# Attention and a Fourier layer on one core: 57 sums of two raw blocks by adding transfers from GpSimd

## The chip, the cores and the metric

One core of a Trainium2 chip runs the whole program. The time is device microseconds (us) for one execution; the program's three runs give 2825.47, 2827.83 and 2831.37 us, median 2827.83.

## What is computed

Two independent layers share the input size (2048 positions, 1024 channels) and are written side by side. All is float32.

```
qkv = x @ wqkv                      # 2048x1024 @ 1024x3072, 32 heads of 32
p   = softmax(q k^T / sqrt(32))     # per head, 2048 x 2048
a   = (p v, heads joined) @ wo      # 2048x1024 @ 1024x1024
u,w = xb @ Wd_re^T, xb @ Wd_im^T    # Fourier layer: along the channels
b   = Ws_re @ u - Ws_im @ w         # along the positions, real part
out = concat(a, b)
```

## The kernel before

**Matmuls.** TensorE (PE) does three products for one float32 product: each operand is split in a high and a low part (float32r), and high x high, low x high and high x low are added in PSUM. `halves` makes the split: line 544 (DVE) or 542 (ACT) copies the block to the high part, line 547 (GpSimd, POOL in the profile, or DVE) subtracts to get the low part. A stationary operand of four 128 x 128 blocks is a piece, tile `hl`, four buffers (`piece`); a moving operand is a tile `slot` (`moving`).

**Seven products in place of eight.** All large products except attention's own are cut 2 x 2 and made by seven block products (numbered 1 to 7) of sums and differences of blocks. So a piece is often a sum of raw blocks: product 5 of the query/key/value stage needs w10 + w11, product 6 needs w10 + w11 - w00. `fetch` makes these sums: it loads the first block into a tile `raw` (or `er`, ten buffers, in the opening; line 506), loads each further block into a second tile (`g`, or `raw` in the opening; line 515), and adds or subtracts it in place with an instruction on POOL or DVE (line 522). Where a later product uses the sum again, it is stored (line 531).

**Stages.** The opening (`qkv`, the first 200 us) makes queries, keys and values of the first three pairs of weight blocks by products 1, 2, 5, 6, 3 in turn; each product takes six groups of 12 matmuls for queries and keys, then eight for values. Results of product 5 are stored group by group (`u_d`, line 820) on SP's queue. Then attention of 32 heads runs from about 210 us to about 2747 us in three streams on PE: S (scores, line 1896, for row maxima on DVE, line 1902, and row sums on ACT, line 1905), T (transposed scores, line 2018, exponentials on ACT, line 2022) and V (line 2037). The rest of the projections and the whole Fourier layer are cut into groups of matmuls, the fills (line 457), that PE does between the streams' steps; the last of them are a tail after attention.

**Who sets the order.** `Plan` simulates the five engines with a cost for every operation (`op`) and lets each engine take, by rank, what is ready. An operation that may run on POOL or DVE goes where it is begun first. POOL's operations and DVE's two-input ones or casts are kept from running at the same time, as the plan reckons. The plan is run 90 times with drawn parameters, and the shortest is written out as each engine's instruction order. On the chip every queue is in order: an instruction that waits holds those behind it. All transfers of before are issued by SP but one; a load that must wait for a buffer, or a store that waits for its result, holds the loads behind it.

**Small rows.** For each head, `scores` makes the row maxima's high and low parts in a tile `lh`, transposes them into `lt` and stores them; both have two buffers.

Of the kernel before, what the change touches and what calls it, by code (L numbers as in the profile page):

```python
# [9 lines left out]
F32 = mybir.dt.float32  # L10
F32R = mybir.dt.float32r
AF = mybir.ActivationFunctionType
ALU = mybir.AluOpType
# [4 lines left out]
P = 128  # L18
# [5 lines left out]
NS = S // P  # L24
# [39 lines left out]
class Plan:  # L64
# [49 lines left out]
    def op(self, engine, cost, emit, after=(), uses=(), rank=0.0, kb=0, order=None, other=None, lanes=1, two=False, wide=False):  # L114

        o = Op(engine, cost, emit, rank, kb, other, two)
        o.lanes, o.wide = lanes, wide
        self.ops.append(o)  # L120
        seen = set()
        for d in after:
            if d is not None and id(d) not in seen:
                seen.add(id(d))
                self._wait(o, d)
        for u in uses:
            u.append(o)
        if order is not None:
            p, order.first = order.first, o
            if p is not None and not p.begun:  # L130
                p.soon.append(o)
                o.left += 1
        return o
# [18 lines left out]
    def start(self, o, e=None):  # L152
        e = e or o.engine
        ins = None
        if not self.dry:
            o.emit(e) if o.other else o.emit()
            ins = self.tc.nc.cur_bb.bb.instructions[-1]
        if not self.dry and e == "POOL" and self.ported[0] > self.now - self.BEHIND:
            self.tc.add_manual_dep(ins, self.ported[1].name, mybir.DependencyInfo(mybir.DependencyClass.Sync, mybir.DependencyReason.DATA), reason="shared port")
        if e == "DVE" and o.two:  # L160
            self.ported = (self.now + (o.cost if e == o.engine else o.other[1]), ins)
        o.begun = True
        self.free[e] = self.now + (o.cost if e == o.engine else o.other[1])
        if e == "POOL" or e == "DVE" and o.two:
            self.port = self.free[e]
        if o.kb:
            for _ in range(o.lanes):
                t = max(self.free[e], self.lane[0])
                self.dma = max(self.dma, t) + o.kb / o.lanes / self.KB_US * (self.WIDE if o.wide else 1.0)
                o.end = self.dma + self.LANDING  # L170
                self.lane = self.lane[1:] + [o.end]
                if o.lanes > 1:
                    self.free[e] = t + o.cost
        else:
            o.end = self.free[e]
            self.free[e] -= self.OVERLAP.get(e, 0.0)
        for t in o.then:
            t.ready = max(t.ready, self.after(o, e, t))
            t.left -= 1
            if t.left == 0:  # L180
                self._release(t)
        for t in o.soon:
            t.ready = max(t.ready, self.now)
            t.left -= 1
            if t.left == 0:
                self._release(t)
# [67 lines left out]
def kernel(  # L254
# [12 lines left out]
    nc = tc.nc  # L267
# [77 lines left out]
    sm = ctx.enter_context(tc.tile_pool(name="sm", bufs=1, reuse_waits="tile"))  # L345
# [42 lines left out]
    MAX, EVAC, CAST, BIT = 1.22, 0.685, 0.415, 0.275  # L388
    SUB = 1.31
    ISSUE = 0.46  # L390

    LATE = 0.25
    HB = 0
# [20 lines left out]
    op = pl.op  # L414
# [69 lines left out]
    def fetch(shape, terms, store=None, keep=None):  # L484

        box = {}
        raws, seconds, tile_of, gate = where[0]
        rank = seq()
        sign, *first = terms[0]
        loaded = len(first) == 2  # L490
        if len(terms) == 1 and not loaded:
            return first[0].get, first[0].made, first[0].users
        if keep is None:
            old, users = raws.take()
        else:

            old, users = gate + keep.users, keep.users

        def dest():
            if "r" not in box:  # L500
                box["r"] = tile_of(shape, "raw", len(raws.users)) if keep is None else keep.get()
            return box["r"]

        last = None
        if loaded:
            last = op("SP", ISSUE, lambda: nc.sync.dma_start(dest(), first[0]), old + first[1] + gate, [users], rank, 256, raws if keep is None else None)
            old = []
        for sign, *term in terms[1:]:
            other = {}
            if len(term) == 2:  # L510
                gold, gusers = seconds.take()

                def load(src=term[0], other=other):
                    other["q"] = tile_of(shape, "g", len(seconds.users))
                    nc.sync.dma_start(other["q"], src)

                q = op("SP", ISSUE, load, gold + term[1] + gate, [gusers], rank, 256, seconds)
            else:
                other["k"], q, gusers = term[0], term[0].made, term[0].users

            def add(e, sign=sign, other=other, a=None if last is not None else first[0]):
                (nc.gpsimd if e == "POOL" else nc.vector).tensor_tensor(  # L522
                    out=dest(), in0=dest() if a is None else a.get(), in1=other["q"] if "q" in other else other["k"].get(), op=ALU.add if sign > 0 else ALU.subtract)

            last = op("POOL", SUB, add, old + [first[0].made if last is None else last, q], [users, gusers] + ([first[0].users] if last is None else []),
                      rank, 0, raws if keep is None and last is None else None, other=("DVE", ADD, 20 + rank), two=True)
            old = []
        if keep is not None:
            keep.made = last
        if store is not None:  # L530
            store[1].append(op("SP", ISSUE, lambda: nc.sync.dma_start(store[0], dest()), [last], [users], rank, 256))
        return dest, last, users
# [1326 lines left out]

    streams = {n: [] for n in "STV"}  # L1860
    psS_r, psT_r, pt_r, vt_r, rt_r, ot_r = Ring(2), Ring(2), Ring(NPT), Ring(2), Ring(1), Ring(2)
    small = {n: Ring(b) for n, b in (("st", 2), ("nm", 2), ("lh", 2), ("tw", 1))}
    qx_r = Ring(1)
    got = {}
    Tops, Sops = {}, {}
# [6 lines left out]
    def scores(h):  # L1872
# [12 lines left out]
        for n, (qt, c) in enumerate([(k % 4, k // 4) for k in range(8)] + [divmod(k, 2) for k in range(8, 32)]):  # L1885
            old, users = psS_r.take()
            own = h > 0 and qt < 4
            box = {}
# [20 lines left out]
            b = op("DVE", MAX, mx, [a] + (sold if n == 0 else []), [users, suse], 0)  # L1909
            e = op("ACT", ES, ex, [b], [users, suse], 0)  # L1910
# [10 lines left out]
        box = {}  # L1921
# [3 lines left out]
            nc.vector.tensor_reduce(out=ST["nm"], in_=ST["negm"].rearrange("p c n -> p n c"), axis=AX.X, op=ALU.min)  # L1925

        def high():
            box["l"] = sm.tile([P, 2, NS], F32R, name="lh", bufs=2)
            nc.vector.tensor_reduce(out=box["l"][:, 0], in_=ST["negm"].rearrange("p c n -> p n c"), axis=AX.X, op=ALU.min)

        def low():
# [3 lines left out]
        a = op("DVE", TINY, nmin, maxes + nold, [nuse, suse], -2)  # L1935
        c = op("DVE", TINY, low, [a, b], [nuse, luse], -2, two=True)
        def across():
            box["t"] = sm.tile([P, 2 * NS], F32, name="lt", bufs=2)
            nc.vector.transpose(box["t"], f(box["l"]).rearrange("p i s -> p (i s)"))

        d = op("DVE", TINY, across, [b, c], [luse], -2)
# [291 lines left out]
```

## Time and profile before

| | |
|---|---|
| three runs, median (range) | 2827.83 us (2825.47 to 2831.37) |
| profiled execution, first to last instruction | 2829.8 us |
| PE busy | 2797.1 us (99%) |
| DVE busy | 2377.2 us (84%) |
| ACT busy | 2355.6 us (83%) |
| POOL busy | 1191.7 us (42%) |
| transfers | 768.18 MB, mean 271 GB/s |

Matmuls are pipelined, so PE's busy time also hides some that start late; the distance between the starts of matmuls tells more. Waits are put down to what came last by the profile. The profiled execution has no other time than its span.

### The profile page before, as it was taken

How to read it: one execution, taken by the hardware profiler on the slowest of the kernel's cores; microseconds unless marked ns; L12 is line 12 of the kernel's file. 1: busy time of each engine (PE TensorE's matmuls, PEld its weight loads, DVE VectorE, ACT ScalarE, POOL GpSimd, SP SyncE). 2: the span in 40 equal slices, each digit the busy share in tenths (PEclk: the TensorE clock that was granted, in tenths of full speed). 3: DMA queues.
4: the chain of work that ended last, by engine and by line, in shares of the span. 5: the costliest groups of instructions: out<-in, count | busy, mean ns of one | idle time of the engine just before them, and what ended most of it. 6: DMA issues, size and time to landing. Idle time of an engine off the chain costs nothing.

```text
span 2829.8 us, 47069 instructions
## 1 busy us (share of the span) xinstructions
PE 2797.1 (99%) x14728; PEld 2095.6 (74%) x14728; DVE 2377.2 (84%) x3300; ACT 2355.6 (83%) x4490; POOL 1191.7 (42%) x945
## 2 busy tenths in 40 slices
PE   9999999999999999999999999999999999999999
PEld 8787777776777777677676777767767777777777
DVE  6678888788888888798988899888888998888845
ACT  5348898998899899889999988999988988888851
POOL 2234434133234432356545446676765331343300
PEclk9999999999999999999999999999999999999999
DMA  9989978798899988977999767888867665677548
GB/s 345 344 312 305 316 249 293 252 337 298 300 302 344 333 298 297 296 232 231 335 342 339 251 207 241 293 270 266 277 179 237 220 211 185 203 237 252 178 154 296
DMA packets 485844, 768.18 MB, mean 271 GB/s; under 512 B 120382, under 2 KB 153406, under 8 KB 485470
## 3 DMA queue, kind: packets, MB, share of 16 engines
q1 hardware_dynamic: 485452, 765.04, 81.6%
q8 instruction: 119, 1.95, 0.3%
q14 instruction: 129, 1.06, 0.1%
q10 hardware_dynamic: 144, 0.13, 0.0%
HBM read 511.74 MB, written 253.25 MB: 270 GB/s over the span
## 4 chain that ended last, share of the span: by engine, by line
PE 88%; DMA 5%; ACT 3%; DVE 2%; issue 1%; POOL 1%; SPq 1%; DVEq 0%; POOLq 0%; ACTq 0%
PE pd L457 40%; PE pd L2037 15%; PE psT L2018 15%; PE psS L1896 14%; PE psT L457 4%; ACT psS L1905 2%; ACT pt L2022 1%; DVE negm L1902 1%; DMA ha_d<-slot 1%; DMA ha_d<-c 0%; DMA c<-in_xb 0%; DMA raw<-in_xa 0%; DMA slot<-in_ct 0%; DMA qs<-qk_d 0%; DMA raw<-in_wv 0%
## 5 line engine op out<-in xcount | busy, mean ns | idle before, releaser
L457 PE MATMUL pd<-slot,hl 128*128 128x512 f32 x5088 | 1412.1, 380 | 4.0 <-ACT hl L542 2.0
L2022 ACT ACTIVATE pt<-psT 128x512 f32<-128x512 f32 x2048 | 1215.3, 689 | 228.8 <-PE psT L2018 227.3
L1902 DVE TENSOR_REDUCE negm<-psS 128x1 f32<-128x1024 f32 x1024 | 1241.5, 1219 | 169.2 <-PE psS L1896 153.8
L1905 ACT ACTIVATE psS<-psS,negm 128x1024 f32<-128x1024 f32 x1024 | 1225.1, 1197 | 41.6 <-DVE negm L1902 40.7
L457 PEld LDWEIGHTS pd<-slot,hl 128*128 128x128 f32 x5088 | 963.8, 190 | 133.3 <-ACT hl L542 2.4
L2018 PE MATMUL psT<-qs,ks 128*128 128x512 f32 x2048 | 786.0, 387 | 1.2 <-DMA r_d<-ll 0.7
L2018 PEld LDWEIGHTS psT<-qs,ks 128*128 128x128 f32 x2048 | 383.2, 188 | 168.8 <-issue 46.9
L1896 PE MATMUL psS<-ks,qs 128*128 128x512 f32 x1552 | 457.9, 381 | 9.1 <-ACT psS L1905 8.9
L2037 PE MATMUL pd<-pt,vt 128*32 128x512 f32 x4096 | 459.3, 594 | 2.8 <-DVE e L766 1.8
L547 POOL TENSOR_TENSOR slot<-raw,slot 128x512 fp32r<-128x512 f32 x153 | 194.9, 1279 | 353.8 <-DVE slot L547 98.8
L547 POOL TENSOR_TENSOR slot<-slot,slot 128x512 fp32r<-128x512 f32 x206 | 260.4, 1280 | 196.3 <-DVE slot L544 50.1
L1896 PEld LDWEIGHTS psS<-ks,qs 128*128 128x128 f32 x1552 | 283.7, 189 | 66.4 <-ACT psS L1905 21.3
L2037 PEld LDWEIGHTS pd<-pt,vt 128*32 128x32 f32 x4096 | 123.9, 110 | 281.4 <-issue 261.3
L1905 ACT ACTIVATION_READ_ACCUMULATOR psS<-psS,negm 128x1 f32 x1024 | 324.8, 317 | 0.0
L522 POOL TENSOR_TENSOR raw<-raw,g 128x512 f32<-128x512 f32 x114 | 145.4, 1279 | 231.9 <-DMA g<-tg_d 23.6
L547 POOL TENSOR_TENSOR hl<-raw,hl 128x512 fp32r<-128x512 f32 x113 | 144.4, 1279 | 214.8 <-PE psT L2018 62.0
L457 PE MATMUL pd<-slot,slot 128*128 128x512 f32 x780 | 200.8, 379 | 0.0
L457 PEld LDWEIGHTS pd<-slot,slot 128*128 128x128 f32 x780 | 147.4, 189 | 20.1
L1896 PE MATMUL psS<-ks,qx 128*128 128x512 f32 x496 | 146.5, 386 | 6.1 <-ACT psS L1905 5.3
L1896 PEld LDWEIGHTS psS<-ks,qx 128*128 128x128 f32 x496 | 90.0, 189 | 34.9 <-ACT psS L1905 10.9
L522 DVE TENSOR_TENSOR raw<-raw,g 128x512 f32<-128x512 f32 x146 | 106.9, 740 | 9.1 <-issue 2.2
L2050 DVE TENSOR_TENSOR ot<-ot,pd 128x512 f32<-128x512 f32 x64 | 43.9, 686 | 68.7 <-PE pd L2037 67.9
(139 smaller groups left out, 2135.0 us busy)
## 6 DMA issues: line engine op xcount, KB each, us to landing
hl<-ha_d SPq DMA_DIRECT2D x134, 512.0 KB
slot<-in_ct SPq DMA_DIRECT2D x144, 256.0 KB
qk_d<-e SPq DMA_DIRECT2D x52, 512.0 KB
qs<-qk_d SPq DMA_DIRECT2D x128, 192.0 KB
ks<-qk_d SPq DMA_DIRECT2D x128, 192.0 KB
raw<-g_d SPq DMA_DIRECT2D x96, 256.0 KB
ha_d<-hl SPq DMA_DIRECT2D x42, 512.0 KB
raw<-in_ct SPq DMA_DIRECT2D x80, 256.0 KB
```

The costliest lines, as they stand in the source:

```text
L457: nc.tensor.matmul(box["ps"], a[1]((a[0].hi, a[0].lo)[u]()), turns((b[0].hi, b[0].lo)[v]()), start=k == 0, stop=k == n - 1)
L522: (nc.gpsimd if e == "POOL" else nc.vector).tensor_tensor(out=dest(), in0=dest() if a is None else a.get(), in1=other["q"] if "q" in other ...
L547: (nc.gpsimd if e == "POOL" else nc.vector).tensor_tensor(out=lo(), in0=raw(), in1=f(hi()), op=ALU.subtract)
L1896: nc.tensor.matmul(p[:, i * NB : i * NB + NB], (QX[0] if own else QS[h % 2])[:, qt * P : qt * P + P], turns(KS[h % 2][:, c * 1024 + i * NB ...
L1902: nc.vector.tensor_reduce(out=ST["negm"][:, c, qt : qt + 1], in_=box["p"], axis=AX.X, op=ALU.max, negate=True)
L1905: nc.scalar.activation(box["p"], box["p"], AF.Exp, bias=ST["negm"][:, c, qt : qt + 1], accum_out=ST["sums"][:, c, qt : qt + 1])
L2018: nc.tensor.matmul(box["p"], KS[h % 2][:, t * P : t * P + P], turns(QS[h % 2][:, j * NB : j * NB + NB]), start=True, stop=True)
L2022: nc.scalar.activation(box["t"], box["p"], AF.Exp)
L2037: nc.tensor.matmul(po["p"][j * DH : j * DH + DH, :], VT[h][:, k, :], box["t"], start=(k == t0), stop=(k == t), tile_position=(0, j * DH),)
L2050: nc.vector.tensor_tensor(out=as_two(po["o"]), in0=as_two(po["o"]), in1=order_of(po["p"]), op=ALU.add)
```

## The change

```diff
@@ Plan.start
-            t.ready = max(t.ready, self.after(o, e, t))
+            t.ready = max(t.ready, self.after(o, "SP" if o.kb else e, t))
...
+    ADDING = 1.0
...
@@ fetch
         for sign, *term in terms[1:]:
             other = {}
+            if len(term) == 2 and sign > 0 and last is not None:
+                last = op("POOL", ADDING, lambda src=term[0]: nc.gpsimd.dma_start(dest(), src, accum_op=ALU.add), [last] + term[1] + gate, [users], rank, 256)
+                continue
             if len(term) == 2:
                 gold, gusers = seconds.take()
...
-    small = {n: Ring(b) for n, b in (("st", 2), ("nm", 2), ("lh", 2), ("tw", 1))}
+    small = {n: Ring(b) for n, b in (("st", 2), ("nm", 2), ("lh", 1), ("tw", 1))}
...
-            box["l"] = sm.tile([P, 2, NS], F32R, name="lh", bufs=2)
+            box["l"] = sm.tile([P, 2, NS], F32R, name="lh", bufs=1)
...
-            box["t"] = sm.tile([P, 2 * NS], F32, name="lt", bufs=2)
+            box["t"] = sm.tile([P, 2 * NS], F32, name="lt", bufs=1)
...
-    nc = bacc.Bacc("TRN2", target_bir_lowering=False, num_devices=1, dynamic_dma_scratch_size=256)
+    nc = bacc.Bacc("TRN2", target_bir_lowering=False, num_devices=1, dynamic_dma_scratch_size=512)
```

In `fetch`, a further block that is loaded and added (not subtracted, and not the first of the sum) no longer goes to a second tile. Once the first block has landed, GpSimd issues a transfer that adds the second block to what lies in the tile. The plan takes 1.0 us of POOL for the issue and gives the transfer the same landing time as one of SP's. 57 sums fit: 24 of the query/key/value weights (14 of them in the opening: eight of the value weights, six of the query/key weights), 8 of the Fourier layer's input, 9 of the last projection and 16 in the Fourier layer's last stage. `lh` and `lt` have one buffer, and the scratch for descriptors that GpSimd writes has 512 bytes a partition, not 256. As the plan reckons with other operations, all engines' orders change; in the changed program lines after 390 stand one lower, after 509 four lower (506 becomes 507, 515 becomes 519, 522 becomes 526, 531 becomes 535, 547 becomes 551, 820 becomes 824), and the adding transfers are line 512.

POOL's queue early in the opening, before; `er` are sums' tiles, `slot` and `hl` low parts of operands, `e` and `vh` the two parts of a finished query/key block:

```order
L547 TENSOR_TENSOR slot3_1016<-er_953,slot3_1016 128x512
L547 TENSOR_TENSOR slot36_1263<-er_1198,slot36_1263 128x512
L522 TENSOR_TENSOR er_1244<-er_1244,raw_1227 128x512
L522 TENSOR_TENSOR er_1268<-er_1268,raw_1258 128x512
L547 TENSOR_TENSOR e_1323<-e_1323,vh_1331 128x512
L547 TENSOR_TENSOR slot39_1347<-er_1268,slot39_1347 128x512
L522 TENSOR_TENSOR er_1446<-er_1446,raw_1334 128x512
L522 TENSOR_TENSOR er_1462<-er_1462,raw_1453 128x512
L547 TENSOR_TENSOR slot1_1533<-er_1462,slot1_1533 128x512
```

and after:

```order
L551 TENSOR_TENSOR slot3_1016<-er_953,slot3_1016 128x512
L512 DMA er_1191<-in_wv 128x512
L512 DMA er_1198<-in_wv 128x512
L512 DMA er_1209<-in_wv 128x512
L551 TENSOR_TENSOR e_1268<-e_1268,vh_1275 128x512
L512 DMA er_1216<-in_wv 128x512
L551 TENSOR_TENSOR slot36_1303<-er_1191,slot36_1303 128x512
L551 TENSOR_TENSOR slot37_1319<-er_1198,slot37_1319 128x512
L551 TENSOR_TENSOR slot39_1355<-er_1216,slot39_1355 128x512
L512 DMA er_1227<-in_wqk 128x512
```

Before, POOL makes two of product 5's value-weight sums (er_1244, er_1268), DVE the others. Now all four are adding transfers, three of them ahead of the low part of `e`.

POOL's queue at product 6 before, whose three query/key pieces are er_1854, er_1931 and er_1972 (the rows name their last subtraction, POOL's share):

```order
L522 TENSOR_TENSOR er_1734<-er_1734,raw_1762 128x512
L547 TENSOR_TENSOR slot13_1831<-er_1734,slot13_1831 128x512
L547 TENSOR_TENSOR slot15_1906<-er_1817,slot15_1906 128x512
L522 TENSOR_TENSOR er_1854<-er_1854,raw_1883 128x512
L522 TENSOR_TENSOR er_1931<-er_1931,raw_1904 128x512
L522 TENSOR_TENSOR er_1972<-er_1972,raw_1950 128x512
L547 TENSOR_TENSOR hl_2049<-er_1972,hl_2049 128x512
L522 TENSOR_TENSOR er_2064<-er_2064,raw_2057 128x512
```

and after, where the pieces are er_1792, er_1901 and er_1938:

```order
L551 TENSOR_TENSOR slot7_1717<-er_1660,slot7_1717 128x512
L512 DMA er_1683<-in_wv 128x512
L512 DMA er_1712<-in_wv 128x512
L512 DMA er_1747<-in_wv 128x512
L512 DMA er_1777<-in_wv 128x512
L512 DMA er_1792<-in_wqk 128x512
L551 TENSOR_TENSOR hl_1905<-er_1792,hl_1905 128x512
L512 DMA er_1901<-in_wqk 128x512
L512 DMA er_1938<-in_wqk 128x512
```

Five adding transfers, four of value weights and one for the first piece, now stand in a row ahead of the first piece's low part; its subtraction has gone to DVE.

SP's queue at the second piece of product 6 (er_1931) before; u_d20 to u_d23 are stores of product 5's groups, one each 12 matmuls:

```order
L820 DMA u_d21_2_592<-e_1878 128x512
L506 DMA er_1894<-in_xa 128x512
L515 DMA raw_1904<-in_wqk 128x512
L531 DMA sv_d3_512<-er_1817 128x512
L820 DMA u_d22_2_595<-e_1900 128x512
L506 DMA er_1921<-in_xa 128x512
L820 DMA u_d23_2_598<-e_1923 128x512
L515 DMA raw_1929<-in_wqk 128x512
L506 DMA er_1931<-in_wqk 128x512
```

and after (er_1901):

```order
L824 DMA u_d21_2_592<-e_1855 128x512
L507 DMA er_1872<-in_xa 128x512
L507 DMA er_1881<-in_xa 128x512
L824 DMA u_d22_2_595<-e_1878 128x512
L535 DMA sv_d3_512<-er_1777 128x512
L507 DMA er_1901<-in_wqk 128x512
L535 DMA sq_d0_501<-er_1792 128x512
L824 DMA u_d23_2_598<-e_1903 128x512
L519 DMA raw_1913<-in_wqk 128x512
```

The load of the second piece's base and one of the two loads of activations (in_xa) now stand ahead of the next u_d store. The first piece's base (er_1792) stands ahead of u_d18, where before (er_1854) it stood behind u_d19, ahead of u_d20; the third's base stands last ahead of the store u_d0_4 in both.

## Prediction

> **What bounds the kernel now.** I read the page first, then the waits of PE, then PE's stretches, then the timeline and the chain of waits around the one stretch of the program's opening in which PE falls back.
>
> ```profile
> span 2829.8 us, 47069 instructions
> PE 2797.1 (99%) x14728; PEld 2095.6 (74%) x14728; DVE 2377.2 (84%) x3300; ACT 2355.6 (83%) x4490; POOL 1191.7 (42%) x945
> ```
>
> PE is the bound: all that any edit outside PE can win is 2829.8 - 2797.1 = 32.7 us of recorded idle time, and what hides in matmuls that run late. The waits of PE name who ended that idle time (total, times, longest):
>
> ```profile
> PE psS L1896 <- ACT psS L1905: 14.2, 23, 2.6
> PE pd L457 <- ACT hl L542: 2.0, 1, 2.0
> PE pd L2037 <- DVE e L766: 1.8, 1, 1.8
> ...
> PE psT L457 <- DVE hl L547: 1.3, 1, 1.3
> PE pd L457 <- POOL hl L547: 1.0, 1, 1.0
> ```
>
> Most of it, 14.2 us, is attention's own loop: a score block waits until ACT has emptied the last one. Raw sums have no part in that. The three rows that end in hl (a weight piece, split in high and low) do: those pieces are what the 57 sums make. They stand in one place, as the stretches show (PE, PEld, DVE, ACT, POOL busy; clock, DMA share, GB/s):
>
> ```profile
> 50.00:100.00 50.00, 50.00 (x233) 43.80 (x232) 35.55 (x48) 17.40 (x30) 12.56 (x10) 1.00 0.97 341
> 100.00:150.00 50.00, 45.45 (x198) 38.12 (x198) 31.81 (x50) 15.30 (x26) 14.34 (x12) 0.97 1.01 351
> 150.00:200.00 50.00, 50.00 (x234) 43.77 (x233) 35.71 (x48) 21.89 (x37) 13.16 (x10) 1.00 0.97 338
> 2700.00:2750.00 50.00, 50.00 (x293) 34.64 (x290) 20.68 (x33) 29.17 (x54) 0.00 (x0) 1.00 0.37 120
> ```
>
> Around 100 to 150 us PE starts 198 matmuls where its neighbours start 233 and 234, with the transfer engines at 0.97 to 1.01 and 338 to 351 GB/s: the opening is as near to transfer-bound as to PE-bound. PE's timeline there (start, length, last the idle time and what ended it):
>
> ```profile
> 109.09 5.34 PE L457 MATMUL psT<-slot,slot 128*128 128x512 f32 x24
> 114.27 2.75 PE L457 MATMUL pd<-slot,slot 128*128 128x512 f32 x12
> 119.02 0.48 PE L457 MATMUL pd<-slot,hl 128*128 128x512 f32 x1 [1.99 <-ACT hl L542]
> 119.83 4.33 PE L457 MATMUL pd<-slot,hl 128*128 128x512 f32 x11 [0.33 <-DVE hl L547]
> 123.99 3.20 PE L457 MATMUL psT<-slot,hl 128*128 128x512 f32 x13
> 128.46 2.64 PE L457 MATMUL psT<-slot,hl 128*128 128x512 f32 x11 [1.27 <-DVE hl L547]
> 130.94 2.97 PE L457 MATMUL pd<-slot,hl 128*128 128x512 f32 x13
> 134.87 2.64 PE L457 MATMUL pd<-slot,hl 128*128 128x512 f32 x11 [0.96 <-POOL hl L547]
> 137.34 2.75 PE L457 MATMUL psT<-slot,hl 128*128 128x512 f32 x12
> ```
>
> Undisturbed, 24 matmuls take 114.27 - 109.09 = 5.18 us, 0.216 each. From 114.27 to 137.34 there are 72 of them: 15.5 us of work in 23.1, so 7.5 us are lost. This is product 6, whose three weight pieces are sums of three blocks. Each of its first additions becomes an adding transfer. It is the one place where the change touches the path that sets the end.
>
> **The change part by part.** *Removed: 57 additions.* They stand in these groups, with others that stay (mean ns of one behind the busy time):
>
> ```profile
> L522 POOL TENSOR_TENSOR raw<-raw,g 128x512 f32<-128x512 f32 x114 | 145.4, 1279 | 231.9 <-DMA g<-tg_d 23.6 <-DVE raw L522 20.4 <-DVE slot L544 16.2
> L522 DVE TENSOR_TENSOR raw<-raw,g 128x512 f32<-128x512 f32 x146 | 106.9, 740 | 9.1 <-issue 2.2 <-DMA raw<-in_wd 1.4 <-DMA raw<-in_xb 1.4
> L522 DVE TENSOR_TENSOR er<-er,raw 128x512 f32<-128x512 f32 x31 | 24.4, 790 | 2.8 <-DMA er<-in_xa 1.0 <-DMA raw<-in_wv 0.8 <-POOL er L522 0.4
> L522 POOL TENSOR_TENSOR er<-er,raw 128x512 f32<-128x512 f32 x13 | 16.6, 1280 | 44.1 <-DMA er<-in_xa 11.4 <-DVE slot L547 9.4 <-DVE er L522 7.0
> ```
>
> At 0.740 on DVE or 1.279 on GpSimd they are 42 to 73 us of busy time. On the path that is next to nothing: if DVE had all 42 of its 2377.2, it would be 1.8% less busy, and 1.8% of the 14.2 us that scores wait behind DVE and ACT is 0.3 us. I take -0.3.
>
> *Moved: 57 issues, from SP to GpSimd.* The issues of one kind of load, and the casts of such tiles on DVE (min/median/max ns, first and last start):
>
> ```profile
> L506 SPq DMA_DIRECT2D er<-in_wv x20: 327/414/981, 5.0 to 135.9; - x20
> L544 DVE CAST slot<-er x7: 417/426/427, 13.7 to 127.4; 128x512 fp32r<-128x512 f32 x7
> ```
>
> SP gets 57 x 0.414 = 24 us back, 14 x 0.414 = 5.8 of them in the opening. SP waits there for stores (the chain below), so I cost this at nothing; what it does is let loads move ahead, counted below. GpSimd gets 57 issues. No row shows a transfer that GpSimd issues. Its bounds are SP's 0.41 and GpSimd's own whole addition, 1.28; I take 1.0, nearer the row of the engine that does it. That is 57 us where the additions would have been up to 73: GpSimd, at 42%, does not become a bound. Its queue is in order, though. The three transfers that now stand together early on hold up the low half of a finished query/key block, for which a store and then the first scores wait; PE has projection matmuls in hand then, so that costs nothing. The five before the first product 6 piece's low half hold up that half; it needs the fifth of them anyway.
>
> The Trainium skill (SBUF — State Buffer, section "SBUF: two separate sides") says that GpSimd cannot write a transfer's descriptors while DVE runs a two-port copy or cast, which speaks against this change. No run here shows it. In this kernel's rows it would hold one issue by at most a cast, 0.43 us, so 1.3 us for the three pieces of product 6.
>
> *Lengthened: each sum's chain.* Before, two loads fly side by side and an addition follows. Now one load lands, GpSimd issues, and a second flight follows. Flights, from the chain of waits (start, length):
>
> ```profile
> 102.58 4.13 DMA raw<-in_wv
> 107.75 2.71 DMA raw<-in_wv
> ...
> 112.56 0.33 SPq L820
> 112.93 4.86 DMA er<-in_xa
> ...
> 189.91 5.88 DMA raw<-in_xa
> ...
> 200.23 2.52 DMA c<-in_xb
> ```
>
> Bounds 2.5 and 5.9; I take 3.9, the mean of the three within the crowded 100 to 115 us. The chain grows by 1.0 + 3.9 - 1.28 = 3.6 us (bounds 0.41 + 2.52 - 1.28 = 1.7 and 1.28 + 5.88 - 0.74 = 6.4).
>
> The Trainium skill (DMA: Bandwidth & Descriptors, section "Anatomy of one DMA — SWDGE (gpsimd) path") gives 2.0 us and bytes / 436e3 for such a transfer, an estimate of 2.6 us for 256 KB. The quiet flights here, 2.5 and 2.7, agree; the crowded ones do not, and they decide. By that rule the chain would grow by 1.3, not 3.6, and the sum below would come out at -1.9 us (0.0 in place of +2.3).
>
> *Where 3.6 us meets slack.* Product 5's third piece:
>
> ```profile
> 78.41 0.64 SPq L506 DMA_DIRECT2D er<-in_wqk  x1
> 83.96 1.28 POOL L522 TENSOR_TENSOR er<-er,raw 128x512 f32<-128x512 f32 x1 [3.88 <-DVE slot L547]
> 86.48 0.62 ACT L542 ACTIVATE hl<-er 128x512 fp32r<-128x512 f32 x1
> 87.22 0.68 DVE L547 TENSOR_TENSOR hl<-er,hl 128x512 fp32r<-128x512 f32 x1
> 88.37 5.34 PE L457 MATMUL psT<-slot,hl 128*128 128x512 f32 x24
> ```
>
> It is ready at 87.90, and PE needs it halfway through the last row, at 88.37 + 12 x 0.216 = 90.96: slack 3.1. Its load loses one neighbour on SP (0.4). So 3.6 is just covered, 6.4 would cost 2.9.
>
> Product 6 has no slack; PE waits for all three pieces. By the order, the first piece's base load moves ahead across two u_d stores, that is two groups of 12 matmuls, 5.2 us; the second's across one, 2.6 us; the third stays before the same store. So the pieces come 3.6 - 5.2 = -1.6, 3.6 - 2.6 = +1.0 and +3.6 us later. These are not added: a wait for one gives the next its time. I take the middle of the last two, +2.3. An activation load also moves ahead across a store. The chain shows such a load (112.93) as what ended the first wait, 1.99 + 0.33 us. It goes; late next is the first piece, 1.6 earlier. That is worth -1.6.
>
> The other 43 sums are hidden: all of PE's waits for an hl piece (4.3 us in the rows above) lie in the 100 to 150 us stretch, so later sums are ready in time. In the tail, with 16 of them, PE has no idle time at 2700 to 2750 and transfers fill 0.37 of it. Six raw buffers there are six pieces of 2.6 us each ahead, against 3.6. Were that cover gone, the stage would start 3.6 us late, once.
>
> *Single copies* of the two row buffers: a head comes every 2829.8 / 32 = 88 us, and the store that must land first flies at most 5.9. Nothing.
>
> Sum: -0.3 + 2.3 - 1.6 = +0.4 us on 2829.8. The profiled execution is its span, 2829.8 us, 2.0 above the median of the runs and within their spread; I carry the difference over: 2827.83 + 0.4 = **2828.2**.
>
> **The rivals.** *A, the opening's hole closes.* Loads start earlier and need fewer buffers; if that feeds product 6 in time, the 7.5 us come back: 2820.3. For it: the loads' new places. Against: the same bytes cross at 338 to 351 GB/s, and adding transfers come on top. Chance 0.15.
>
> *B, adding transfers are slow in the crowded opening.* They also read what lies in SBUF. If that takes engine time like a second transfer, each costs 262,144 B / 345 GB/s = 0.76 us more, 14 of them 10.6 in a stage without room. Or the chain grows by the upper bound: 6.4 at product 6 and 2.9 at product 5, less the 1.9 gained, 7.4 together. I price it between the two, at 9.0: 2836.8. It decides from issue plus flight of about 7.5 us on: the growth g is then 6.2, and the losses (g - 1.3) + (g - 3.5), less 1.9, are 5.7. For it: no cover at product 6. Against: 3 of the 14 lie on the path. Chance 0.20.
>
> *C, the change does little and the new order does the rest.* The planner reckons every time anew, so all five engines' orders shift, far from any sum. The 23 waits of attention, 14.2 us, then fall elsewhere; half of them more or less is 7.1 us: 2820.7 or 2834.9. Chance 0.10 faster and 0.08 slower.
>
> **How the numbers follow.** What is left, 0.47, is the forecast. Its own range is 2822.5 to 2834, the 0.2% (5.7 us) that a measurement of this kernel, whose runs spread over 5.9 us, can tell from no change. Faster: A and C, 0.25. Slower: B and C, 0.28. The range goes from A's 2820 to just past B's, 2838.
>
> **What would show it.** Right: the hole at 114 to 137 us still there, 6 to 11 us deep, its pieces waiting for a transfer that GpSimd issued; GpSimd's issues near 1 us; landings 2.5 to 6 us later; PE's other waits within a few us of 14.2. Wrong: PE without idle time before 140 us (A); issue plus flight over 7.5 us, waits for adding transfers at product 5 or in the tail (B); attention's waits changed by over 5 us (C).

## The result: 85 us slower

| | before | after |
|---|---|---|
| median (range), four runs each | 2828.15 us (2825.47 to 2831.37) | 2913.05 us (2911.62 to 2914.87) |
| profiled execution, span | 2829.8 us | 2910.2 us |
| PE busy, mean granted clock | 2797.1 us, 0.998 | 2822.9 us, 0.991 |

The ratio is 1.0296 (95% interval 1.0283 to 1.0308). The forecast was 2828.2 us in a range of 2820 to 2838, so the result lies far outside it. The page after, first the span and the engines:

```profile
span 2910.2 us, 47016 instructions
PE 2822.9 (97%) x14728; PEld 2106.3 (72%) x14728; DVE 2380.9 (82%) x3267; ACT 2367.3 (81%) x4506; POOL 1191.4 (41%) x962
```

The span is 80.4 us longer. PE's idle time went from 32.7 to 2910.2 - 2822.9 = 87.3 us, 54.6 more. The other 25.8 are busy time: the same 14728 matmuls took longer. The granted clock fell by 0.7%, which is 20 of 2823 us. The waits of PE after, by line (total, times, longest):

```profile
PE psS L1900 <- ACT psS L1909: 23.8, 31, 3.4
PE pd L458 <- ACT hl L546: 13.1, 1, 13.1
PE psT L2022 <- ACT pt L2026: 10.3, 4, 5.2
PE psT L2022 <- DMA qs<-m_d: 7.6, 4, 3.5
```

One wait for a weight piece (hl) grew from 2.0 to 13.1 us, and attention's waits for its own scores, exponentials and row maxima grew too, though attention has no raw sums. The place tells more than the releaser. Five stretches of PE's time before (PE, PEld, DVE, ACT, POOL busy; clock, DMA share, GB/s):

```profile
0.00:100.00 100.00, 98.54 (x442) 85.53 (x443) 71.36 (x105) 48.87 (x83) 22.20 (x21) 1.00 0.98 344
100.00:200.00 100.00, 95.45 (x430) 81.90 (x430) 67.52 (x97) 37.19 (x62) 27.50 (x22) 0.98 0.99 345
300.00:400.00 100.00, 98.47 (x524) 73.60 (x517) 85.48 (x119) 87.03 (x169) 39.83 (x32) 1.00 0.85 280
900.00:1000.00 100.00, 100.00 (x543) 74.76 (x542) 88.02 (x116) 88.90 (x171) 42.70 (x34) 1.00 0.98 341
2700.00:2800.00 100.00, 100.00 (x524) 78.43 (x521) 47.89 (x75) 41.35 (x74) 1.28 (x1) 1.00 0.59 192
```

The same five after:

```profile
0.00:100.00 100.00, 92.90 (x407) 79.44 (x408) 63.68 (x92) 46.63 (x81) 23.68 (x24) 0.98 0.95 322
100.00:200.00 100.00, 82.06 (x352) 69.65 (x351) 53.02 (x78) 28.70 (x47) 25.87 (x22) 0.90 0.93 289
300.00:400.00 100.00, 88.49 (x466) 61.64 (x455) 76.58 (x105) 75.62 (x146) 41.03 (x35) 0.97 0.89 281
900.00:1000.00 100.00, 90.69 (x452) 67.03 (x453) 85.40 (x110) 81.49 (x155) 36.95 (x31) 0.95 0.94 309
2700.00:2800.00 100.00, 89.81 (x467) 62.69 (x466) 59.66 (x82) 66.08 (x127) 28.66 (x27) 0.95 0.60 141
```

PE's idle time in these 500 us is 56.05 us after and 7.54 before: 48.5 of the 54.6 us. Of all stretches of 100 us only these five have a clock below 1.00. Adding transfers stand in each of them, though also in places that lose less (2249 to 2332 us). Two groups of the adding line (ns min/median/max, first and last start), then what their engine waited for and their landing:

```profile
L512 POOL DMA_DIRECT2D raw<-s_d x16: 872/888/903, 2681.4 to 2772.3; - x16
L512 POOL DMA_DIRECT2D raw<-in_wqk x10: 865/880/1140, 280.7 to 396.2; - x10
...
  issue: 79.0, 19
...
DMA to landing us min/median/max: 3.9/5.0/7.5
```

Issue (0.89) and landing (5.0 with the issue) are as forecast, 1.0 and 4.9. New is "issue: 79.0, 19": 19 times GpSimd stood, 4.2 us each, at an adding transfer for which nothing in the profile was missing. That row shows only a part, since other waits are put down to whatever the profile saw last. By the starts and landings in the trace, 35 of the 57 adding transfers begin 0.26 to 0.32 us after the one before has landed, with 137.4 us of GpSimd's idle time ahead of them, and none begins earlier. GpSimd's timeline in the opening shows it (start, length, last the idle time before it and what ended it):

```profile
105.33 0.89 POOL L512 DMA_DIRECT2D er<-in_wv  x1
111.56 0.87 POOL L512 DMA_DIRECT2D er<-in_wv  x1 [5.34 <-DVE acc L718]
118.50 0.88 POOL L512 DMA_DIRECT2D er<-in_wv  x1 [6.06 <-issue]
124.08 1.00 POOL L512 DMA_DIRECT2D er<-in_wv  x1 [4.70 <-issue]
130.97 0.88 POOL L512 DMA_DIRECT2D er<-in_wqk  x1 [5.89 <-issue]
137.88 1.26 POOL L551 TENSOR_TENSOR hl<-er,hl 128x512 fp32r<-128x512 f32 x1 [6.02 <-ACT hl L546]
```

And PE's there, the hole of product 6:

```profile
122.00 2.75 PE L458 MATMUL pd<-slot,slot 128*128 128x512 f32 x12
137.85 0.80 PE L458 MATMUL pd<-slot,hl 128*128 128x512 f32 x1 [13.10 <-ACT hl L546]
139.19 4.42 PE L458 MATMUL pd<-slot,hl 128*128 128x512 f32 x11 [0.55 <-POOL hl L551]
...
150.13 5.70 PE L458 MATMUL psT<-slot,hl 128*128 128x512 f32 x12 [3.92 <-DVE hl L548]
```

Adding transfers begin 5.6 to 6.9 us apart, each 0.31 or 0.32 us after the one before has landed. The fifth in this line, which begins at 130.97, is the first piece of product 6; PE waits 13.10 us for it. After waits PE is near half speed: the twelve matmuls behind the wait of 3.92 us take 5.70 us, where twelve took 2.75 before the hole. From 130 to 140 us the clock granted to PE is 0.50.

### The profile page after: what moved, and what is told of

It is laid out like the page before. It is cut to its first block, busy times and chain, and to the rows that moved or that the text cites. A ratio compares the mean times of both kernels' runs of the same rounds, so it can differ in the third digit from the quotient of the medians.

```text
span 2910.2 us, 47016 instructions
## 1 busy us (share of the span) xinstructions
PE 2822.9 (97%) x14728; PEld 2106.3 (72%) x14728; DVE 2380.9 (82%) x3267; ACT 2367.3 (81%) x4506; POOL 1191.4 (41%) x962
## 3 DMA queue, kind: packets, MB, share of 16 engines
q0 software_dynamic: 8208, 14.95, 3.4%
## 4 chain that ended last, share of the span: by engine, by line
PE 80%; DMA 6%; issue 5%; ACT 4%; DVE 3%; POOL 2%; SPq 1%; POOLq 0%; DVEq 0%; ACTq 0%
PE pd L458 36%; PE pd L2041 14%; PE psT L2022 14%; PE psS L1900 13%; PE psT L458 3%; ACT psS L1909 2%; DVE negm L1906 1%; ACT pt L2026 1%; DMA qs<-m_d 1%; DMA er<-in_wqk 0%; DMA raw<-in_ct 0%; DMA er<-in_wv 0%; DMA slot<-in_ct 0%; POOL slot L551 0%; DMA slot<-tg_d 0%
## 5 line engine op out<-in xcount | busy, mean ns | idle before, releaser
L458 PE MATMUL pd<-slot,hl 128*128 128x512 f32 x5112 | 1434.0, 382 | 21.0 <-ACT hl L546 13.1
L458 PEld LDWEIGHTS pd<-slot,hl 128*128 128x128 f32 x5112 | 975.1, 191 | 153.9 <-ACT hl L546 13.5
L1900 PE MATMUL psS<-ks,qs 128*128 128x512 f32 x1552 | 460.7, 384 | 19.2 <-ACT psS L1909 15.5
L551 POOL TENSOR_TENSOR slot<-slot,slot 128x512 fp32r<-128x512 f32 x202 | 255.4, 1277 | 202.2 <-DVE slot L548 36.7
L1909 ACT ACTIVATION_READ_ACCUMULATOR psS<-psS,negm 128x1 f32 x1024 | 314.0, 307 | 0.0
L551 POOL TENSOR_TENSOR slot<-raw,slot 128x512 fp32r<-128x512 f32 x146 | 188.3, 1302 | 270.8 <-ACT slot L546 80.8
L526 POOL TENSOR_TENSOR raw<-raw,g 128x512 f32<-128x512 f32 x108 | 138.8, 1289 | 133.3 <-issue 10.3
L526 DVE TENSOR_TENSOR raw<-raw,g 128x512 f32<-128x512 f32 x109 | 80.9, 751 | 27.2 <-DMA raw<-t_d 6.1
```

Source lines behind the costliest of these rows:

```text
L458: nc.tensor.matmul(box["ps"], a[1]((a[0].hi, a[0].lo)[u]()), turns((b[0].hi, b[0].lo)[v]()), start=k == 0, stop=k == n - 1)
L526: (nc.gpsimd if e == "POOL" else nc.vector).tensor_tensor(out=dest(), in0=dest() if a is None else a.get(), in1=other["q"] if "q" in other ...
L551: (nc.gpsimd if e == "POOL" else nc.vector).tensor_tensor(out=lo(), in0=raw(), in1=f(hi()), op=ALU.subtract)
L1900: nc.tensor.matmul(p[:, i * NB : i * NB + NB], (QX[0] if own else QS[h % 2])[:, qt * P : qt * P + P], turns(KS[h % 2][:, c * 1024 + i * NB ...
L1909: nc.scalar.activation(box["p"], box["p"], AF.Exp, bias=ST["negm"][:, c, qt : qt + 1], accum_out=ST["sums"][:, c, qt : qt + 1])
```

## What the experiments tested

Theory R: the change gives GpSimd's transfer descriptors a store of 512 bytes a partition, which holds one adding transfer; the next, and GpSimd's whole queue behind it, stands until that one has landed. Rivals: L, only the chain of first load, second transfer, sum is longer; D, an adding transfer takes more DMA time for its bytes; P, GpSimd can't write descriptors while VectorE uses their common port; A, adding itself goes one at a time; N, the new plan is an unlucky one; later Q, GpSimd's issues and queue alone.

**The moves by themselves, with two stores.** Two programs of moves only, alike but for this line:

```diff
-SCRATCH = 512
+SCRATCH = 4096
```

> This kernel leaves the whole computation out: it only moves blocks, in phases that follow each other (8 plain loads by SP; 8 plain loads by GpSimd; 8 adding transfers of 128 rows of 2 KB; 4 adding transfers to one tile, each after the last has landed; 8 adding ones of 64 rows, of 32 rows, of 128 rows of 512 B; 8 of 128 rows while VectorE copies without a pause; 8 beside 24 plain loads by SP). The descriptor store is that of the changed kernel, 512 bytes a partition. Theory R (the store of 512 bytes holds the descriptors of one adding transfer of 128 rows, so the next begins only when it has landed): adding transfers of 128 rows begin 4 to 6 us apart, of 512-byte rows also one at a time (3 to 5 us), of 64 rows up to three begin within 1 us of each other before one waits, of 32 rows six. Theory L (transfers of their own are free to overlap, only the landing of 5.0 us is long): starts 0.9 to 1.0 us apart in every phase, landing 4 to 5 us. Theory P (GpSimd cannot write descriptors while VectorE uses their common port): starts 0.9 us apart in the quiet phases and several us apart only beside VectorE's copies. Theory A (adding itself goes one at a time): 4 to 6 us apart in all adding phases, whatever the rows, and the plain loads by GpSimd 1 us apart.

> The same program of moves, with a descriptor store of 4096 bytes a partition. R: adding transfers of 128 rows now begin 0.9 to 1.0 us apart in all phases (eight of them fit), and the eight land within some 8 to 10 us where one at a time took 35 to 45. L: nothing changes against the store of 512 bytes. P: nothing changes. A: nothing changes, 4 to 6 us apart.

With 512 bytes, GpSimd's timeline: eight plain loads (line 38, the first rows), eight adding ones of 128 rows of 2 KB (line 42), eight of 64 rows (line 49):

```profile
33.06 1.80 POOL L38 DMA_DIRECT2D U<-in_wv  x3 [32.62 <-DVE U L29]
36.31 1.24 POOL L38 DMA_DIRECT2D U<-in_wv  x2 [1.44 <-issue]
...
49.45 0.90 POOL L42 DMA_DIRECT2D T<-in_wv  x1 [8.69 <-DVE T L29]
53.84 0.88 POOL L42 DMA_DIRECT2D T<-in_wv  x1 [3.49 <-issue]
58.16 0.87 POOL L42 DMA_DIRECT2D T<-in_wv  x1 [3.44 <-issue]
...
108.40 2.54 POOL L49 DMA_DIRECT2D A<-in_wv  x3 [6.64 <-DVE A L29]
111.65 0.81 POOL L49 DMA_DIRECT2D A<-in_wv  x1 [0.72 <-issue]
```

With 4096 bytes, the adding ones of 128 rows, and the same while VectorE makes one copy after the other (line 61):

```profile
48.05 7.08 POOL L42 DMA_DIRECT2D T<-in_wv  x8 [10.79 <-DVE T L29]
...
128.24 7.93 POOL L61 DMA_DIRECT2D U<-in_wv  x8 [6.13 <-DVE U L29]
```

One at a time, 4.3 us apart, becomes eight in 7.08 us. With the small store three transfers of 64 rows begin without a pause before one waits, as R said; those of 512-byte rows (a quarter of the bytes, as many rows) went one at a time too, 3.0 us apart, and eight of 32 rows never waited (a wait after six was expected). Beside 24 plain loads by SP, adding ones began 4.0 to 7.6 us apart with the small store, and all eight in 7.11 us with the large one. R is shown for the moves. L, A and P fall as causes of the spacing: beside VectorE's copies an issue takes 0.11 us longer and isn't held. The Trainium skill (SBUF — State Buffer, section "SBUF: two separate sides") lets GpSimd write no descriptors during VectorE's two-port copies; 80 copies of 0.427 us (median), with 0.03 us between them on average, did not hold these eight, and the measurement decides.

**The store alone, in the kernel.** The room for a larger store had to be made first:

```diff
-NPT = 25
+NPT = 24
...
-ahead = (Ring(10), RAW, ... name="er", bufs=10) ...
+ahead = (Ring(9), RAW, ... name="er", bufs=9) ...
```

ring512 is that; ring2048 is that and

```diff
-dynamic_dma_scratch_size=512
+dynamic_dma_scratch_size=2048
```

> The changed kernel with nine raw buffers in the opening where it has ten and 24 probability buffers in the attention where it has 25, which frees the room for the next run; the store stays at 512 bytes. It is the control. All theories: near the changed kernel, 2895 to 2930 us, since one buffer of each ring is worth little; adding transfers 4 to 7 us apart where they stand together.

> The control with a descriptor store of 2048 bytes and nothing else: the order of the instructions on every engine is the same, row for row. R: adding transfers that are ready begin about 1 us apart, GpSimd's queue behind them isn't held, and 50 to 75 of the 85 us come back: 2840 to 2865 us. L (only the chain from the first load to the sum is longer, 5.0 us where the plan has 2.4): no change, within 5 us of the control. D (an adding transfer takes about twice the DMA time of a plain one, 1.74 against 0.79 us on each of 16 engines): no change. N (the new plan is just a worse one): no change.

ring512: 2900.9 us, ratio to before 1.0258 (1.0242 to 1.0273), 12 us below the changed kernel with the same store; the buffers and their new plan make that. ring2048: 2855.0 us, 1.0100 (1.0083 to 1.0117). No instruction changed its place, and 46 us are gone, somewhat under the 50 to 75 expected. What GpSimd stood for at the adding line with nothing missing, with 512 bytes and with 2048:

```profile
  issue: 62.3, 19
```

```profile
  issue: 14.0, 6
```

And the engines in the same order:

```profile
PE 2823.4 (97%) x14728; PEld 2101.2 (72%) x14728; DVE 2382.8 (82%) x3281; ACT 2361.7 (81%) x4492; POOL 1190.9 (41%) x962
```

```profile
PE 2804.2 (98%) x14728; PEld 2101.2 (74%) x14728; DVE 2370.3 (83%) x3281; ACT 2358.6 (83%) x4492; POOL 1192.0 (42%) x962
```

In ring2048, 31 of the 57 adding transfers begin while the one before is still in flight; in ring512 none does. So R is the cause of these 46 us. GpSimd's busy time is the same within 1.1 us. PE's idle time falls from 2899.8 - 2823.4 = 76.4 to 2848.9 - 2804.2 = 44.7 us, and its matmuls take 19.2 us less, at a clock of 0.998 in place of 0.988.

**The order alone.** serial512 keeps the change's store and buffers and tells the plan what the moves showed:

```diff
+                if e == "POOL":
+                    self.store = o.end
...
+        if e == "POOL" and self.store > self.now >= self.port:
+            for x in sorted(able):
+                if not x[3].kb and not x[3].begun:
...
-                o.end = self.dma + self.LANDING
+                o.end = self.dma + self.LANDING + (2.0 if e == "POOL" else 0.0)
```

> The changed kernel with its buffers and its store of 512 bytes, and a plan that is told all that the moves showed: the longer landing, twice the DMA time, and that a second adding transfer can't begin before the one before has landed, so that it puts GpSimd's other work between them. If most of the loss is GpSimd's queue standing behind an adding transfer that waits for the store, and the order can avoid it, 40 to 70 of the 85 us come back: 2843 to 2873 us. If the loss is in the rate itself (fourteen sums in the opening can't be had at one per 5 us), less than 25 us come back: above 2888 us.

2869.6 us, 1.0147 (1.0131 to 1.0162): 43 us come back. GpSimd's standing at the adding line, and four of the five stretches:

```profile
  issue: 76.3, 19
```

```profile
100.00:200.00 100.00, 86.00 (x376) 73.24 (x377) 60.23 (x86) 31.18 (x51) 21.38 (x19) 0.92 0.96 312
300.00:400.00 100.00, 100.00 (x542) 74.40 (x541) 86.13 (x118) 89.93 (x174) 46.30 (x39) 1.00 0.92 283
900.00:1000.00 100.00, 99.85 (x534) 71.78 (x534) 89.06 (x120) 90.90 (x175) 35.47 (x27) 1.00 0.96 328
2700.00:2800.00 100.00, 99.80 (x543) 72.81 (x541) 48.07 (x80) 66.25 (x122) 12.01 (x13) 1.00 0.58 152
```

By this row GpSimd stands as often as with the change. By the landings it stands less: 25 adding transfers begin just as the one before has landed, with 93.3 us of idle time ahead of them, where 35 had 137.4. Outside the opening these are 63.3 and 104.9 us, and PE hardly suffers for them any more: the losses at 300, 900 and 2700 us are gone, and PE's idle time after the first 200 us is 32.9 us, against 62.2 with the change and 26.6 before. In the opening, where 14 sums are wanted within some 105 us, the order wins little (14.0 us idle against 17.9 from 100 to 200 us).

**Opening or not.** rest_only:

```diff
-if len(term) == 2 and sign > 0 and last is not None:
+if len(term) == 2 and sign > 0 and last is not None and len(raws.users) != 10:
```

> The changed kernel with the opening's 14 sums made as before, by a load into a second buffer and an addition, and the other 43 by adding transfers. The milestones of the trace put 25 to 30 us of the loss in the opening and some 55 after it. If the loss is local to the places where adding transfers stand (R), this is 45 to 60 us above the kernel before: 2873 to 2888 us. If the opening's delay is what everything later suffers from, it is within 20 us: below 2848 us.

2884.4 us, 1.0203 (1.0182 to 1.0224): 56 us of loss stay without the opening's 14, as R's local losses say.

**Buffers and plans.** base924 is the kernel before with the nine and 24 buffers; noadd2048 is ring2048 with the condition of the new branch made false, the whole change without its transfers; seed2_2048 is ring2048 with `random.Random(2)` in the search.

> The kernel before with nine raw buffers in the opening and 24 probability buffers, no adding transfer: what the two runs with other stores gave up to make room. If the buffers and the new plan they bring (N) are what is left of the loss with the larger store, this is 15 to 30 us above the kernel before (2843 to 2858 us). If what is left is the adding transfers' own chain and DMA time (L, D), it is within 5 us of it (2823 to 2833 us).

> The kernel with the store of 2048 bytes with every sum made as before, by a load into a second buffer and an addition: it keeps the single row buffers, nine raw buffers and 24 probability buffers, so that it is the whole change without its transfers. If the single row buffers and a new plan make what is left of the loss with the larger store (N): 2845 to 2860 us. If the adding transfers themselves do (D or L): 2825 to 2836 us, as the kernel with nine and 24 buffers alone.

> The kernel with the store of 2048 bytes and all 57 adding transfers, its plan drawn with other random numbers. N (what is left is the luck of one plan): it moves by 8 us or more from 2855 us, either way. D or L: within 6 us of it.

base924: 2833.3 us, 1.0013 (1.0002 to 1.0024). noadd2048: 2832.1 us, 1.0016 (1.0007 to 1.0025). seed2_2048: 2849.7 us, 1.0076 (1.0061 to 1.0091). Buffers, single row copies and store cost some 4 us. The 85 us are, in this order, 12 from the changed kernel to ring512, 46 for the store, 23 for the transfers with a large store (and the plan made with them), and these 4. N falls as the cause of the whole: the two plans with all 57 are 18 to 23 us above the kernel without, and differ by 5 from each other. What differs by 5 us or so between two plans isn't read below, and told2048 shows that a plan can do more.

**What is left with a large store, 18 to 23 us.** told2048 is ring2048 with serial512's line on LANDING, and 512 KB where the plan counts 256 (serial512 has that too); rest2048 is ring2048 with rest_only's edit, for its ring of nine:

> The kernel with the store of 2048 bytes, and a plan that is told what an adding transfer takes: the DMA time of 512 KB where it counted 256, and a landing 2 us later, which makes some 6 us from issue to landing where it counted 3.4. If what is left of the loss comes from a plan made on a landing that is too early (sums expected before they are there, work queued behind them), this is 10 to 25 us faster than with the store alone: 2830 to 2845 us. If it comes from the longer chain itself or from the buffers, it stays at 2850 to 2858 us.

> The store of 2048 bytes, and adding transfers for the 43 sums outside the opening only. D (the adding transfers' double DMA time costs where the DMA engines are full, above all in the opening, 98 to 99% busy; 14 times 0.95 us more): 8 to 14 us faster than with all 57, that is 2841 to 2847 us. N or L: as with all 57, 2850 to 2859 us, or anything else that follows no place.

told2048: 2867.6 us, 1.0140 (1.0123 to 1.0156), slower than untold. rest2048: 2852.4 us, 1.0085 (1.0069 to 1.0100), the same as all 57 within a plan's luck. told2048 lies outside both of its ranges, rest2048 in the one of N or L. The plan's early landing isn't what is left; why the better-told plan is 12.6 us worse was not tried. For rest2048 PE's idle time says more than the total: in the first 200 us it is 6.1 us, as before (6.0), against 11.0 in ring2048, and after them 40.4 against 33.7. So the opening's part does come back, and more than that is lost again later, for a cause that isn't shown.

Then each suspect alone, added to noadd2048 (2832.1 us). DMA time, by a transfer from DRAM to DRAM beside each of the opening's 14 sums, or each of the other 43:

```diff
+                if len(raws.users) == 9 and sign > 0 and last is not None:
+                    op("SP", ISSUE, lambda src=term[0], n=len(spent): nc.sync.dma_start(spare_d[n], src), term[1], [], rank, 256)
```

> The kernel without adding transfers, with one more plain transfer of 256 KB beside each of the opening's 14 sums, from DRAM to DRAM, for which nothing waits. It adds DMA time and nothing else (about 0.8 us on each of 16 engines, 11 us in all, against 13 us that the adding ones add there). D: 6 to 12 us slower than without them. If the opening has DMA time to spare: within 3 us of it.

> The kernel without adding transfers, with one more plain transfer of 256 KB from DRAM to DRAM beside each of the 43 sums outside the opening; nothing waits for it, and the plan counts it. It has the DMA time alone (about 0.6 to 0.8 us on each engine each, 26 to 34 us in all). D: 10 to 20 us slower, 2842 to 2852 us. L or Q: within 5 us, 2827 to 2837 us.

The chain, by a second load that waits for the first:

```diff
-q = op("SP", ISSUE, load, gold + term[1] + gate, [gusers], rank, 256, seconds)
+behind = [last] if sign > 0 and last is not None else []
+q = op("SP", ISSUE, load, gold + term[1] + gate + behind, [gusers], rank, 256, seconds)
```

> The kernel without adding transfers (2832.1 us), where the second load of each of the 57 sums waits until the first has landed, as an adding transfer must; the addition stays VectorE's or GpSimd's. It has the longer chain without the double DMA time and without GpSimd's issues. L: 10 to 25 us slower, 2842 to 2857 us. D or Q: within 5 us, 2827 to 2837 us.

GpSimd's queue, by a second load that it issues (`q = op("POOL", ADDING, load, ...)`, with `nc.gpsimd` in `load`), and ring2048 with adding transfers for the last 25 sums only:

> The kernel without adding transfers, where the second load of each of the 57 sums is a plain transfer that GpSimd issues; it waits for nothing but its buffer, and the addition stays. It has GpSimd's issues and queue without the chain and without the double DMA time. Q: 10 to 20 us slower, 2842 to 2852 us. D or L: within 5 us, 2827 to 2837 us.

> The store of 2048 bytes, and adding transfers for the last 25 sums only (of output weights, attention's output and sequence sums, after 2200 us), where the DMA engines are 55 to 75% busy. D: within 4 us of the kernel without adding transfers (2828 to 2836 us), since the DMA time is to be had there. L: half of what is left comes with 25 of 57, 2839 to 2846 us.

| | us | ratio to before (95%) | above noadd2048, us |
|---|---|---|---|
| dummy14, DMA time in the opening | 2844.3 | 1.0055 (1.0038 to 1.0072) | 12.2 |
| dummy43, DMA time elsewhere | 2847.8 | 1.0083 (1.0060 to 1.0106) | 15.7 |
| chain57, the chain | 2839.8 | 1.0049 (1.0033 to 1.0065) | 7.7 |
| gploads57, the queue | 2834.9 | 1.0029 (1.0019 to 1.0038) | 2.8 |
| late2048, 25 late adding ones | 2837.4 | 1.0031 (1.0020 to 1.0042) | 5.3 |

D's stand-ins have the largest numbers in both places, the chain a smaller one, a little under the 10 us that L expected at least. The queue alone is within a plan's luck, so Q falls. The late ones cost little where the engines are 55 to 75% busy (5.3 us, where D expected at most 4 and L half of what is left). But each row is one plan, and each stand-in of D also takes an issue on SP's queue, so the totals don't show this ranking. In the opening PE's idle time supports it: in the first 200 us it is 6.8 us in noadd2048, 13.7 in dummy14, 7.5 in chain57 and 11.0 in ring2048. After them it is 25.1, 29.3, 30.7 and 33.7 us, and 36.7 in dummy43. The parts add up to more than the whole, and no run has the chain and the DMA time together without the adding, so how the 18 to 23 us divide between D and L stays open. No kernel here beats the one before.

D's size, from the queues' shares of 16 engines' span (packets, MB, share): ring2048, then the kernel without adding transfers, then the one with plain loads by GpSimd.

```profile
q1 hardware_dynamic: 477244, 750.09, 79.7%
q0 software_dynamic: 8208, 14.95, 3.2%
```

```profile
q1 hardware_dynamic: 485452, 765.04, 81.4%
```

```profile
q0 software_dynamic: 4560, 14.95, 1.7%
```

57 adding transfers took 0.032 x 2848.9 = 91.2 us of each engine, 1.60 each. The 57 plain loads that they replace took 0.814 x 2832.9 - 0.797 x 2848.9 = 35.4, or 0.62 each; as plain loads by GpSimd 0.017 x 2829.9 / 57 = 0.84. So an adding transfer takes some 1.9 to 2.6 times the DMA time of a plain one of the same bytes.

## Why the prediction was wrong

**The failed step: "That is 57 us where the additions would have been up to 73: GpSimd, at 42%, does not become a bound."** It counted what GpSimd executes, and took for granted that a second adding transfer can begin when the first is issued. It can't with this store: each holds the next for 4 to 7 us, so the 57 are a series of up to 285 us (57 x 5.0) in bursts, not 57. GpSimd's busy share stayed at 41%, and that said nothing. The diff does have the store's size in it, doubled; the prediction gave it no term. ring2048 against ring512 is this step's price: 46 us.

**"Its queue is in order, though ... so that costs nothing"** saw what is queued and priced it by the wrong hold. The first scores, which PE was to bridge with projection matmuls, do wait:

```profile
74.62 1.65 PE L1900 MATMUL psS<-ks,qs 128*128 128x512 f32 x3 [3.52 <-DMA ks<-qk_d]
```

The chain that ends this wait goes back, over the load and store of a query/key block, to the fourth early adding transfer, which begins 0.3 us after the third has landed. Before, PE has no wait from 30 to 100 us, and in ring2048 the first scores don't wait either. serial512 shows the same price outside the opening: with other instructions behind its waits GpSimd still stands 63 us there, and PE's idle time after the first 200 us is 6 us above that of before, not 36.

**"The other 43 sums are hidden"** failed. rest_only has only these, and loses 56 us; "six pieces of 2.6 us each ahead" covers a chain that is 3.6 us longer, not a series at 5 us per sum. With a large store and without adding transfers, the chain alone (chain57) is 7.7 us above noadd2048, in one plan, where the prediction had nothing outside product 6.

**Right were sizes of single things.** Issue 0.89 against 1.0; issue to landing 5.0 against 4.9, in part by luck, since it holds with one in flight at a time (with the larger store the median is 6.4); the single row copies and buffers nearly nothing; the place of the hole, product 6, whose idle time is 13.10 + 0.55 + 3.92 = 17.6 us where "6 to 11 us deep" was named. With the larger store PE's idle time from 115 to 145 us is 2.02 + 0.87 + 3.86 + 0.18 + 0.75 = 7.7 us, against 2.81 + 1.50 + 0.96 = 5.3 without adding transfers: 2.4 more, where the terms +2.3 and -1.6 gave 0.7. The later pieces came about as late as the +2.3 says (3.86 + 0.18 against 1.50 for the second), but the first wait is no shorter (2.02 + 0.87 against 2.81), so the -1.6 did not come. The -0.3 for fewer additions is below what these runs can tell. Two readings were off without weight for the sum: 14.2 us are the largest row of PE's 32.7 us of idle time, not most of it, and attention's heads come every 79 us ((2747 - 210) / 32), not 88.

**Rivals.** B had the right side and engine time near enough (0.76 more each; 0.76 to 0.98 by the shares above; 10.6 us for the opening's 14, 12.2 with the stand-ins of dummy14), but it was confined to the opening and to 9 us, and its deciding point, "issue plus flight of about 7.5 us", was reached by no transfer but the slowest (median 5.0, longest 7.5). Its wait at product 5 did come (1.04 + 0.24 us at 98 us), but through the wait ahead of the issue. A never happened: PE waits longer before 140 us. C's sign came, attention's wait for its scores went from 14.2 to 23.8 us, but not by a new order alone: with one and the same order it is 22.2 us in ring512 and 12.3 in ring2048. C's 7.1 us either way was of the right size for what a new plan does (a seed 5 us, ring512's plan 12), and small beside the cause.

The estimate of 2.6 us that the prediction made from the Trainium skill (DMA: Bandwidth & Descriptors, section "Anatomy of one DMA — SWDGE (gpsimd) path") is under what the moves gave: from the start of the issue, plain loads by GpSimd landed after 2.9 to 3.4 us with the small store, adding ones of 128 rows after 3.9 to 4.2.

## What to carry to other kernels

Where a transfer moves to a queue whose descriptors are made by an engine, ask how many can be in flight before asking how long one takes: two issued back to back in a few lines of their own show it. An engine's busy share doesn't show a queue that stands. The row "issue" among what it waited for does in part, and the start of each transfer beside the landing of the one before does in full; what stands behind them in the order sets the price. And when a planner writes the order, a resource that it doesn't know can cost wherever it puts two users together.

## What the runs showed of the hardware

- The store of 512 bytes a partition held one adding transfer of 128 rows of 2 KB, three of 64 rows, three plain loads of 256 KB. The packets of GpSimd's queue fit a limit, which is an inference: 144 for each adding one (8208 / 57), 80 for each plain one (4560 / 57), so three plain ones, 240, went in and two adding ones, 288, did not.
- A long wait of PE cost twice here: the clock granted around its end was lower. It was 0.50 from 130 to 140 us, at the end of the wait of 13.10 us, and 0.90 in the 100 us with it; a quarter to a third of the 80 us is matmuls that run slower.
- A transfer for which nothing waits can have a price: with 14 of them in the opening, where the DMA share before is 0.98 to 0.99, the kernel took 12.2 us longer, in one plan, and PE's idle time in the first 200 us went from 6.8 to 13.7 us.
